# Taps of two channel chunks by small per-channel products, masks as wide products, and a new written-out order

## The chip, the cores and the metric

The kernel runs on one core of one Trainium2 chip. The metric is device time in microseconds (us) of one execution; lower is better. Three runs of the kernel before gave 263.95, 261.83 and 264.04, so its median is 263.95 us. One more execution, which took 262.47 us, was profiled.

## The reference

Two blocks stand one behind the other, each with its own LayerNorm and residual. Sequence length is 2048, model width D 512, state N 128, hidden width F 1376, batch 1.

```
dt = exp(log_dt);  logdA = dt*(A_re + 1j*A_im)
P  = exp(logdA[:, :, None] * l)                 # l = arange(2048), rounded to bf16
K  = einsum("dn,dnl,dn->dl", C, P, dt*B).real   # one filter of 2048 taps per channel
y  = irfft(rfft(u, 4096) * rfft(K, 4096))[:2048] + u*Dskip   # u = LN(x), a causal convolution
h  = x + y
z  = LN(LN(h));  g = gelu(z @ w1 + b1)
out = h + g @ w2 + b2
```

## The kernel before, in words

**Channels and stages.** The 512 channels are worked in four chunks (NCH) of 128. The filter taps are not computed one by one: a position l is split into a coarse part of NA = 20 entries (ROWS, table A) and a fine part of NB = 33 entries (table B), and a tap is a sum over the 128 states of a product of an A entry and a B entry, real part minus imaginary part. The stages, in the order of the data:

- *Small tables.* Inputs are loaded, transposed on TensorE (L712, L746), and turned into decay rates (th, L720 to L729), magnitudes (logarithms and exponentials on ACT, helper AC, L583) and phases (psi, gam). Helpers record the vector work, so one line stands for many operations: TS is L559 (DVE form) and L561 (tables and masks), TT is L571, STT is L576, evac copies a PSUM slot on ACT (L513) or on DVE (L515). A high and a low f16 half of each phase is made by split() (L685).
- *Exponentials.* bexps (L732) writes table B's magnitudes for all chunks, aexps (L941, L945; L949, L952) table A's.
- *Phases.* chain() adds phases step by step on PSUM (L986), ACT takes sine and cosine (L988), and DVE multiplies the magnitudes by them (L1006 to L1008, and L993, L994 for table A of chunks 2 and 3). It is called four times: B and A of chunks 0 and 1 (hf = 0), then B and A of chunks 2 and 3 (hf = 1). Each step of a chain waits for the sines of the step before.
- *Taps.* kgen (chunks 0 and 1): for each channel two products of 128x20 by 128x33 (L1030, L1031), four channels side by side in the array's columns; a chunk takes 256 of them and two evictions. kgen4 (chunks 2 and 3): four channels in one product of 128x128 by 128x132 (L1061, L1062), of which the diagonal blocks are used; a chunk takes 64 products and six evictions of up to 792 elements. For it table A of these chunks lies in another order (EA2, IA2, through dmaj), padded from 20 to 32 entries: a memset (L1301) zeroes the padding of one half and a DMA (L1339) copies it to the other.
- *Filter spectrum.* kspec (L1095) multiplies the taps by seven twiddle tables W[0..6], which are a sine table times row masks (28 products, L1318, on POOL or DVE); the result goes out to AK_d in device memory and comes back with its axes exchanged (kstage), and fstage (L912) transforms it on.
- *Input spectrum.* LayerNorm statistics (L871), normalized x in UN (L881), xspec (L893), fstage.
- *Product and back.* inverse() multiplies the spectra on DVE (L1135), transforms back (L1145), and a DMA transpose (turn, L1151) puts the result in place.
- *MLP.* tail() (L1214) adds the convolution to x and normalizes twice; mlp() multiplies by w1 (L1268), takes gelu on ACT (L1270), multiplies by w2 (L1290), and adds (L1292) and stores.

**What sets the order.** Nothing is scheduled by the compiler. Every operation is put on a list with its engines, its cost and its dependencies (Sched.add); ORDER (L166 to L203) is a list written out by hand that names the operations in the order in which they are issued, a negative number meaning the second engine that the operation allows. Sched.run walks that list, gives each operation its place on its engine, hands out the four PSUM slots, and puts filler matmuls (L1379) where it reckons that PE would idle. It also counts PE's instructions in blocks of 256, from 193 (L338 to L345). Each engine then works through its own list in order. SyncE (SP) issues nearly all transfers from one queue, in order too.

Of the kernel before, what the change touches and what calls it, by code (L numbers as in the profile page):

```python
# [384 lines left out]
def kernel(ctx, tc, A_u, A_A_re, A_A_im, A_B_re, A_B_im, A_C_re, A_C_im, A_log_dt, A_Dskip,  # L385
# [63 lines left out]
    EB0 = E0 + 2 * ASZ
    BA0 = E0 + 2 * ASZ + NCH * BSZ  # L450
    IB0 = BA0 + 2 * ASZ
    IA2 = at(BA0 + 2 * ASZ + NCH * BSZ, bf16, 2, 4, 32, 32)
    EA2 = at(IA2.hi, bf16, 2, 4, 32, 32)
    pos[0] = EA2.hi
    HF = 2 * ASZ + 2 * BSZ
# [18 lines left out]
    Kg = [take(bf16, NB, 2, 32), at(sc0 - 512, bf16, NB, 4, 2, 32)]
    zlo = take(bf16, NB, 2, 32).lo
    AK0 = take(bf16, 16, 2 * CW).lo
    XB = [at(lo + 16384, bf16, 8, 512) for lo in (E0, BA0)]
    PR = [[at(rest0 + 2048 * n, bf16, 8, CW) for n in range(4)], [take(bf16, 8, CW) for _ in range(2)] + [at(lo + 24576, bf16, 8, CW) for lo in (E0, BA0)]]
    Z = [[at(lo, bf16, P, 16) for lo in q] for q in ((zlo, sc0 + 8192), (EA2.lo + 11264, IA2.lo + 11264))]
# [1 line left out]
    EA = [at(E0 + c * ASZ, bf16, NA, CW) for c in range(2)]
    EB = [at(EB0 + c * BSZ, bf16, NB, CW) for c in range(NCH)]
    IA = [at(BA0 + c * ASZ, bf16, NA, CW) for c in range(2)]
    IB = [at(IB0 + c * BSZ, bf16, NB, CW) for c in range(NCH)]
# [935 lines left out]
```

## Time and profile before

| | |
|---|---|
| median of three runs | 263.95 us (261.83 to 264.04) |
| the profiled execution | 262.47 us |
| its span in the profile | 260.1 us |
| busy: PE / DVE / ACT / POOL | 230.3 / 183.3 / 176.8 / 61.8 us |
| share of the chain that ended last: PE / DVE / ACT | 57% / 25% / 11% |
| granted TensorE clock | 1.00 |

How to read the lines that follow. A line of the timeline has the start and the length in us, the engine, the line of the kernel, the operation with what it writes and reads, the count, and in brackets how long the engine sat idle before it and who released it. A group line has the busy time and the mean in ns of one instruction. A line of the windows has, per engine, its busy time in that stretch with the count of instructions, then the clock, the busy share of the DMA engines, and GB/s. PE is the matmul stream and PEld the weight loads that overlap it. "issue" is time in which an engine waited for nothing that the profile shows. Short matmuls overlap one another, so the time of one is read from the distance of their starts.

### The profile page before, as it was taken

How to read it: one execution, taken by the hardware profiler on the slowest of the kernel's cores; microseconds unless marked ns; L12 is line 12 of the kernel's file. 1: busy time of each engine (PE TensorE's matmuls, PEld its weight loads, DVE VectorE, ACT ScalarE, POOL GpSimd, SP SyncE). 2: the span in 40 equal slices, each digit the busy share in tenths (PEclk: the TensorE clock that was granted, in tenths of full speed). 3: DMA queues.
4: the chain of work that ended last, by engine and by line, in shares of the span. 5: the costliest groups of instructions: out<-in, count | busy, mean ns of one | idle time of the engine just before them, and what ended most of it. 6: DMA issues, size and time to landing. Idle time of an engine off the chain costs nothing.

```text
span 260.1 us, 7656 instructions
## 1 busy us (share of the span) xinstructions
PE 230.3 (89%) x3236; PEld 133.7 (51%) x3249; DVE 183.3 (70%) x368; ACT 176.8 (68%) x214; POOL 61.8 (24%) x234
## 2 busy tenths in 40 slices
PE   7215997888997999989999998899999999999994
PEld 3102673454876586444467765555553434444452
DVE  3999997999999964679899778974615676222021
ACT  2679989999977977578989956966514701762700
POOL 9930871699996000000000000000000000000000
PEclk9999999999999999999999999999999999999999
DMA  6940012000001247729835985560771040214202
GB/s 161 211 108 2 4 38 28 3 4 3 3 5 57 72 164 222 249 93 283 279 112 88 143 161 176 97 170 3 117 131 36 0 93 20 61 28 96 69 15 66
DMA packets 40371, 23.88 MB, mean 92 GB/s; under 512 B 25649, under 2 KB 37778, under 8 KB 40338
## 3 DMA queue, kind: packets, MB, share of 16 engines
q1 hardware_dynamic: 39746, 22.95, 36.8%
q10 hardware_dynamic: 592, 0.46, 0.8%
q8 instruction: 25, 0.41, 0.6%
q14 instruction: 8, 0.07, 0.1%
HBM read 10.03 MB, written 6.29 MB: 63 GB/s over the span
## 4 chain that ended last, share of the span: by engine, by line
PE 57%; DVE 25%; ACT 11%; issue 5%; POOL 0%; DVEq 0%; ACTq 0%; POOLq 0%
PE ps L1268 15%; PE ps L1290 15%; PE ps L1145 8%; PE ps L893 5%; ACT ar L988 4%; ACT ar L513 4%; DVE ar L871 4%; PE ps L912 4%; DVE ar L1007 3%; DVE ar L576 3%; DVE ar L571 2%; PE ps L1095 2%; PE ps L1061 2%; DVE ar L1008 2%; DVE ar L559 2%
## 5 line engine op out<-in xcount | busy, mean ns | idle before, releaser
L513 ACT CAST ar<-ps 128x1024 bf16<-128x1024 f32 (+3 forms) x72 | 65.2, 970 | 19.3 <-PE ps L1145 6.9
L1270 ACT ACTIVATE ar<-ps,ar 128x512 bf16<-128x512 f32 (+1 forms) x44 | 28.2, 686 | 36.7 <-PE ps L1268 36.6
L561 POOL TENSOR_SCALAR ar<-ar 128x128 bf16<-128x128 bf16 (+6 forms) x44 | 39.6, 921 | 7.6 <-ACT ar L583 7.3
L1290 PE MATMUL ps<-ar 128*128 128x512 bf16 (+3 forms) x180 | 39.1, 367 | 0.4
L1268 PE MATMUL ps<-ar 128*128 128x512 bf16 (+1 forms) x176 | 39.3, 379 | 0.0
L515 DVE CAST ar<-ps 128x1024 bf16<-128x1024 f32 (+2 forms) x28 | 30.6, 1113 | 11.9 <-ACT ar L513 4.0
L988 ACT ACTIVATE ar<-ps 128x1024 bf16<-128x1024 int16 x36 | 35.1, 1032 | 5.1 <-DVE ar L1007 1.6
L1135 DVE TENSOR_TENSOR ar<-ar 128x1024 bf16<-128x1024 bf16 x48 | 30.7, 687 | 10.3 <-PE ps L1145 9.9
L1292 DVE TENSOR_TENSOR ar<-ps,ar 128x512 bf16<-128x512 f32 (+1 forms) x17 | 11.1, 660 | 37.7 <-PE ps L1290 35.0
L1290 PEld LDWEIGHTS <-ar 128*128 128x128 bf16 (+1 forms) x187 | 17.9, 98 | 20.0 <-issue 0.8
L1268 PEld LDWEIGHTS <-ar 128*128 128x128 bf16 (+1 forms) x176 | 17.3, 100 | 20.5 <-issue 0.8
L986 PE MATMUL ps<-ar 128*32 128x256 f16 x560 | 21.4, 275 | 5.0 <-ACT ar L988 3.1
L1145 PEld LDWEIGHTS <-ar 64*128 64x128 bf16 x768 | 21.6, 94 | 5.4 <-issue 3.0
L1145 PE MATMUL ps<-ar 64*128 64x128 bf16 x768 | 23.9, 217 | 0.3 <-ACT ar L513 0.3
L986 PEld LDWEIGHTS <-ar 128*32 128x32 f16 x560 | 14.3, 97 | 12.5 <-issue 12.2
L912 PE MATMUL ps<-ar 128*64 128x512 bf16 (+1 forms) x160 | 17.7, 342 | 1.2 <-DMA ar<-AK_d 0.6
L732 ACT ACTIVATE ar<-ar 128x1024 bf16<-128x1024 f32 x16 | 15.6, 1041 | 3.2 <-DVE ar L559 3.2
L893 PE MATMUL ps<-ar 128*32 128x512 bf16 x256 | 16.0, 381 | 0.3 <-ACT ar L513 0.3
L576 DVE SCALAR_TENSOR_TENSOR ar<-ar 128x4 f32<-128x4 f32 (+5 forms) x44 | 14.2, 327 | 2.5 <-ACT ar L583 1.4
L583 ACT ACTIVATE ar<-ar 128x512 f32<-128x512 f32 (+8 forms) x18 | 11.9, 681 | 4.9 <-DMA ar<-in_A_log_dt_dram 1.8
L1008 DVE TENSOR_TENSOR ar<-ar 128x1024 bf16<-128x1024 bf16 x21 | 14.6, 719 | 0.0
L1007 DVE TENSOR_TENSOR ar<-ar 128x1024 bf16<-128x1024 bf16 x21 | 14.5, 716 | 0.1
(99 smaller groups left out, 318.6 us busy)
## 6 DMA issues: line engine op xcount, KB each, us to landing
ar<-AK_d SPq DMA_DIRECT2D x8, 512.0 KB, 5.6
ar<-in_A_u_dram SPq DMA_DIRECT2D x4, 512.0 KB, 9.2
AK_d<-ar SPq DMA_DIRECT2D x2, 1024.0 KB, 4.6
AK_d<-ar SPq DMA_DIRECT2D x4, 512.0 KB, 4.0
out_dram<-ar SPq DMA_DIRECT2D x30, 64.0 KB, 2.0
...
ar<-ar SPq DMA_DIRECT2D x1, 768.0 KB, 5.4
```

Of the source, the lines that this page charges most:

```text
L513: act.copy(out_fn(), in_fn())
L515: dve.tensor_copy(out_fn(), in_fn())
L561: en.tensor_scalar(a, b, f(s1), f(s2), op0, op1)
L893: pe.matmul(pst(p)[32 * cg:32 * cg + 32, 512 * z:512 * z + 512], lhsT=BD.ap()[:, 32 * f + 2 - 2 * jl:32 * f + 34 - 2 * jl], rhs=un[2 * (2 ...
L912: pe.matmul(pst(p)[64 * h:64 * h + 64, w * (k + r):w * (k + r) + w], lhsT=T.ap()[:, f, r, :], rhs=v[f:f + 1].ap()[:, 0, :], start=True, st ...
L986: pe.matmul(pst(p)[32 * g:32 * g + 32, 256 * j:256 * j + 256], lhsT=W2[DELTAS.index(d)].ap(), rhs=S2[g].ap()[:, ch0:ch0 + 256], start=Fals ...
L988: add("ACT", c_act(1024), lambda e, p=p, sc=sc, cs=cs: act.activation(swo(sc[cs]) if hf and kind == "B" else sc[cs].ap().rearrange("p a b ...
L1135: dve.tensor_tensor(o, a, b_[:, :, ::-1, :] if sw else b_, ALU.mult)
L1145: pe.matmul(pst(p)[:, 512 * h + 128 * k:512 * h + 128 * k + 128], lhsT=q.ap()[rows, 2 * k + r, :], rhs=TP[w].ap()[rows, f0 // 2 + k, :], s ...
L1268: pe.matmul(pst(p)[:fs, 512 * z:512 * z + 512], lhsT=w1s[dc].ap()[:, fc * P:fc * P + fs], rhs=ybuf.ap().rearrange("p (t c) k -> p c t k", ...
L1270: add("ACT", c_act(512, 1), lambda e, p=p, z=z, fc=fc, fs=fs: act.activation(hT.ap()[:fs, fc, :], pst(p)[:fs, 512 * z:512 * z + 512], ACT. ...
L1290: pe.matmul(pst(p)[:, 512 * z + c0:512 * z + c1], lhsT=hT.ap()[:fs, fc, 128 * t:128 * t + 128], rhs=w2s[fc].ap()[:fs, c0:c1], start=(fc == ...
```

## The change

It replaces kgen4 by kgen for chunks 2 and 3, so every chunk's taps come from per-channel products of 128x20 by 128x33, and the A tables of all chunks have one layout. With it go the padding memset and the padding DMA, the second arrangement of the sines (swo, swi), and the special multiplications of L993 and L994. The masks become one expanded table (mskx) and seven products of 512 elements in place of 28 of 128. Copies in split() and a few others may run on ACT as well as DVE (CP), and so may the normalization of x. One of two phase tables for TP goes; its third sine is taken in two halves from the first. The two Dskip additions of a pair of chunks become one. Buffers are laid out anew. ORDER is replaced as a whole (1,045 entries before, 1,000 after), and the cost of one case in Sched.run is raised by 0.3.

The core of the diff:

```diff
-    th = tL(f32, 5, 256)
...
-    TT(th[2], p, dtb, ALU.mult, n=256, ...)
-    add("DVE", c_dve(256, 1, True), th3, r=[p, dtb], w=[th[3]], hv=0)
-    TT(th[4], p, dtb, ALU.mult, n=256, ...)
-    TS(th[0:2], th[2:4], -1.0, None, ALU.mult, n=512, pr=0.35)
+    th = tM(f32, 4, 256)
+    for hf in range(2):
+        TT(th[2 + hf], p, dtb, ALU.mult, n=256, ...)
+        CP(th[hf], th[2 + hf], -1.0, pr=0.35)
...
+    def CP(o, i, m=1.0, n=None, iap=None, pr=None):
+        n = n if n is not None else (o.hi - o.lo) // SZ[o.dt]
+        def fn(e):
+            x = iap() if iap else i.ap()
+            if e == "ACT":
+                act.activation(o.ap(), x, ACT.Copy, scale=m)
+            else:
+                dve.tensor_scalar(o.ap(), x, m, None, ALU.mult)
+        add(("DVE", "ACT"), (c_dve(n, 2) + 0.02, c_act(n)), fn, r=[i], w=[o], pr=pr)
...
     def split(x, hl, pr, m=1.0):
-        TS(hl[0], x, m, None, ALU.mult, pr=pr)
+        CP(hl[0], x, m, pr=pr)
...
+    mskx = ct(bf16, 7, 4, 32)
+    mx = lambda e: (dve.tensor_copy if e == "DVE" else gp.tensor_copy)(mskx.ap()..., msk[0:28].ap().unsqueeze(2).to_broadcast([P, 28, 32]))
+    add(("POOL", "DVE"), (5.1, 1.0), mx, r=[msk], w=[mskx], pr=1.55, hv=1)
...
     for v in range(7):
-        for g in range(4):
-            PTS(W[v], valW, msk[4 * v + g:4 * v + g + 1], n=128, ...)
+        TT(W[v], valW, mskx[v], ALU.mult, n=512, mode=2, ..., eng="POOL")
...
-    add("DVE", 1.0, lambda e: dve.memset(pads(EA2), 0.0), w=[EA2], pr=0)
-    dma("SP", lambda: pads(IA2), lambda: pads(EA2), 786432, [EA2], [IA2], pr=3.45)
...
-            (kgen if q == 0 else kgen4)(c, 5.1 + 4 * c)
+            kgen(c, 5.1 + 4 * c)
+        add("DVE", c_dve(64), lambda e, q=q: dve.tensor_tensor(Kg[q][0].ap(), Kg[q][0].ap(), Dz[2 * q:2 * q + 2].ap(), ALU.add), ...)
...
-            add("DVE", c_dve(512, 4) + 0.13, ufn, r=[hs[8 * b + j], nw[3], nw[4]], w=[un[j]], ...)
+            add(("DVE", "ACT"), (c_dve(512, 4) + 0.13, c_act(512, 2)), ufn, r=[hs[8 * b + j], nw[3], nw[4]], w=[un[j]], ...)
```

In the kernel after, the lines that answer to those above are: products of the chain L985 and L986 (L984 their negation), phase matmuls L970 with the sines L972, taps L1008 and L1009, kspec L1045, xspec L886, fstage L905, inverse L1095 (matmuls) and L1085 (products), evac L500 (ACT) and L502 (DVE), w1 L1218, w2 L1240, fillers L1330.

More of the change, by code (lines that the diff above doesn't have):

```diff
@@ L321, in run @@
                     if a <= s < b:
-                        s, end = b, b + c
+                        s, end = b, b + c + 0.3
                 late = [a for a, _ in hold if s < a < end]
@@ L447 @@
     ASZ, BSZ = NA * CW * 2, NB * CW * 2
+    HF, A0 = 2 * ASZ + 2 * BSZ, 2 * ASZ
     E0 = pos[0]
[L449 to L455, printed above, removed]
+    BA0 = E0 + 2 * HF
+    pos[0] = BA0 + 2 * HF
     hs = [at(pos[0] + 1024 * n, bf16, 512) for n in range(16)]
     X0s = V(ar, pos[0] + 16384, bf16, (8, 512))
-    X0 = at(BA0 + HF, bf16, 16, 512)
+    X0 = at(BA0 + 2 * HF - 16384, bf16, 16, 512)
     pos[0] += 24576
@@ L473 @@
     XR = [VS(X0, c) for c in range(NCH)]
[L474 to L479, printed above, removed]
+    Kg = [at(pos[0], bf16, NB, 2, 32), at(sc0, bf16, NB, 2, 32)]
+    zlo = Kg[0].lo + 4224
+    WR = pos[0] + 11264
+    pos[0] = WR + 21248
+    AK0 = WR + 12288
+    X1 = at(E0, bf16, 16, 512)
+    PR = [[at(rest0 + 2048 * n, bf16, 8, CW) for n in range(4)], [at(BA0 + 26624 + 2048 * n, bf16, 8, CW) for n in range(4)]]
+    Z = [[at(lo, bf16, P, 16) for lo in q] for q in ((zlo, sc0 + 8448), (E0 + 16384, BA0 + 4096))]
     assert pos[0] <= NBYTES, pos[0]
[L481 to L484, printed above, removed]
+    EA, IA = ([at(lo + A0 * (1 - (c >> 1)) + ASZ * (c & 1), bf16, NA, CW) for c in range(NCH)] for lo in (E0, BA0))
+    EB, IB = ([at(lo + 2 * A0 + BSZ * c, bf16, NB, CW) for c in range(NCH)] for lo in (E0, BA0))
     ALL = slice(None)
@@ L540, in __call__ @@
             return v
-    tE = Tmp(BA0, BA0 + HF)
-    tL = Tmp(BA0 + HF, IA2.hi)
+    tE = Tmp(BA0 + A0, BA0 + A0 + HF)
+    tL, tM = Tmp(BA0 + A0 + HF, BA0 + 2 * HF), Tmp(BA0, BA0 + A0)
     ct = tL
@@ L595 @@
             dma("ACT", lambda: ldt.ap(), lambda: A_log_dt.partition_broadcast(P), 131072, [], [ldt], pr=0)
+    dtb = tE(bf16, 512)
     xv = x_dram.rearrange("(b q j h l) d -> b h q j (l d)", b=2, j=4, h=2, l=2)
@@ L621 @@
     NF = len(FLD)
-    fi, fsh, fmk = ct(i32, NF), ct(i32, NF), ct(i32, NF)
-    fm, fa, fv = ct(f32, NF), ct(f32, NF), ct(f32, NF)
+    fi, fsh, fmk = tE(i32, NF), tE(i32, NF), tE(i32, NF)
+    fm, fa, fv = tE(f32, NF), tE(f32, NF), ct(f32, NF)
     def fld_fn():
@@ L700 @@
     S.pr = 0.2
-    dtb = tE(bf16, 512)
     AC(dtb, ldt, ACT.Exp, tbl=True)
@@ L748 @@
         pas.append(lambda p=p, n=n: nat(pst(p, bf16)[:, 512 * n:512 * n + 512]))
-    crt, cit = tE(bf16, 512), tE(bf16, 512)
+    crt, cit = tL(bf16, 512), tL(bf16, 512)
     evac(by4(crt), pas[0], 512, [p], [crt])
@@ L781 @@
     S.pr = 0.5
-    psi, gam, wq, ps256 = tL(f32, 512), gr, tL(f32, 512), s2
+    psi, gam, wq, ps256 = tM(f32, 512), gr, tM(f32, 512), s2
     p, pa = tr("aim")
@@ L794 @@
     S.pr = 1.5
-    TPc = [at(Kg[0].lo, i32, 8, P), at(Kg[0].lo + 4096, i32, 8, P)]
+    TPc = at(Kg[0].lo, i32, 8, P)
     codD = ct(i32, 2, 16)
@@ L819 @@
     add("DVE", c_dve(928), lambda e: dve.tensor_reduce(msk.ap(), R.ap(), mybir.AxisListType.X, ALU.add), r=[R], w=[msk], pr=1.55)
+    mskx = ct(bf16, 7, 4, 32)
+    mx = lambda e: (dve.tensor_copy if e == "DVE" else gp.tensor_copy)(mskx.ap().rearrange("p v g c -> p (v g) c"), msk[0:28].ap().unsqueeze(2).to_broadcast([P, 28, 32]))
+    add(("POOL", "DVE"), (5.1, 1.0), mx, r=[msk], w=[mskx], pr=1.55, hv=1)
     wi = ct(i32, 4, 16)
@@ L872 @@
     stats(st, nw, 16, 1.0, EPS, 1.25, ln=True)
-    UN = [[X0s[j] for j in range(7)] + [at(zlo + 1024 * b, bf16, 512)] for b in range(2)]
+    UN = [X0s[j] for j in range(8)]
     def unorm(b, pr):
-        un = UN[b]
+        un = UN
         for j in range(8):
@@ L880, in ufn @@
                 sc_, bi_ = nw[3].ap()[:, s:s + 1], nw[4].ap()[:, s:s + 1]
-                dve.tensor_scalar(un[j].ap(), hs[s].ap(), sc_, bi_, ALU.mult, ALU.add)
-            add("DVE", c_dve(512, 4) + 0.13, ufn, r=[hs[8 * b + j], nw[3], nw[4]], w=[un[j]], pr=pr + 0.001 * (j // 4))
+                if e == "DVE":
+                    dve.tensor_scalar(un[j].ap(), hs[s].ap(), sc_, bi_, ALU.mult, ALU.add)
+                else:
+                    act.activation(un[j].ap(), hs[s].ap(), ACT.Identity, bias=bi_, scale=sc_)
+            add(("DVE", "ACT"), (c_dve(512, 4) + 0.13, c_act(512, 2)), ufn, r=[hs[8 * b + j], nw[3], nw[4]], w=[un[j]], pr=pr + 0.001 * (j // 4))
     def xspec(b, X, pr):
-        S.pr, un = pr, UN[b]
+        S.pr, un = pr, UN
         for f0 in range(0, 16, 2):
@@ L947, in aexps @@
                 add("PE", 1.75 if n < 3 else 0.88, fn, r=[HLt] + [WA[LV.index(LD[4 * n + j])] for j in range(4)] + ([HLg, Ih] if n < 3 else []), w=[p], new=[p] if n < 3 else [])
-                if hf == 0:
-                    add("ACT", c_act(1024), lambda e, p=p, n=n: act.activation(multi(E0 + 4 * n * 256, ASZ, bf16, 2, 4, CW).rearrange("p c a d -> p a c d"), pst(p).rearrange("p (a c d) -> p a c d", a=4, c=2), ACT.Exp),
-                        r=[p, TBL], w=[EA[c][4 * n + z] for c in range(2) for z in range(4)])
-                else:
-                    add("ACT", c_act(1024), lambda e, p=p, n=n: act.activation(dmaj(EA2, 4 * n).rearrange("p x a i -> p a x i"), pst(p).rearrange("p (a x i) -> p a x i", a=4, x=8), ACT.Exp),
-                        r=[p, TBL], w=[EA2])
+                add("ACT", c_act(1024), lambda e, p=p, n=n, hf=hf: act.activation(multi(EA[2 * hf].lo + 4 * n * 256, ASZ, bf16, 2, 4, CW).rearrange("p c a d -> p a c d"), pst(p).rearrange("p (a c d) -> p a c d", a=4, c=2), ACT.Exp),
+                    r=[p, TBL], w=[EA[2 * hf + c][4 * n + z] for c in range(2) for z in range(4)])
     nch = [0]
-    swo = lambda v: v.ap().rearrange("p a (c i g) -> p (a c) i g", c=2, g=4)
-    swi = lambda p: pst(p, i16).rearrange("p (b g i two) -> p b i g two", g=4, i=32, two=2)[:, :, :, :, 0]
     def chain(hf, kind, pr):
-        dm = hf == 1 and kind == "A"
         ch0 = 256 * hf
@@ L987, in chain @@
                 add("PE", 0.55 + (0 if gn else 0.45 if kind == "B" else 1.3), fn, r=[W2, S2, Wm, cst] + ([HLo, I16] if kind == "A" and gn == 0 else []), w=[p], new=[p] if gn == 0 else [])
-                add("ACT", c_act(1024), lambda e, p=p, sc=sc, cs=cs: act.activation(swo(sc[cs]) if hf and kind == "B" else sc[cs].ap().rearrange("p a b -> p (a b)"), swi(p) if hf and kind == "B" else pst(p, i16).rearrange("p (n two) -> p n two", two=2)[:, :, 0], ACT.Sin, scale=SINSC), r=[p, TBL], w=[sc[cs]])
+                add("ACT", c_act(1024), lambda e, p=p, sc=sc, cs=cs: act.activation(sc[cs].ap().rearrange("p a b -> p (a b)"), pst(p, i16).rearrange("p (n two) -> p n two", two=2)[:, :, 0], ACT.Sin, scale=SINSC), r=[p, TBL], w=[sc[cs]])
             mark = [("cg", kind, hf, gn)]
-            if dm:
-                E_, I_ = (lambda b0=b0: dmaj(EA2, b0)), (lambda b0=b0: dmaj(IA2, b0))
-                f_ = [lambda sc=sc, z=z: sc[z].ap().rearrange("p a (x i) -> p x a i", x=8) for z in range(2)]
-                add("DVE", c_dve(1024, 2), lambda e, E_=E_, I_=I_, f_=f_: dve.tensor_tensor(I_(), E_(), f_[0](), ALU.mult), r=[EA2, sc[0]], w=[IA2])
-                add("DVE", c_dve(1024, 2), lambda e, E_=E_, f_=f_: dve.tensor_tensor(E_(), E_(), f_[1](), ALU.mult), r=[EA2, sc[1]], w=[EA2] + mark)
-                continue
             Sx, Cx = (lambda sc=sc: sc[0].ap().rearrange("p e (c d) -> p c e d", c=2)), (lambda sc=sc: sc[1].ap().rearrange("p e (c d) -> p c e d", c=2))
@@ L1316 @@
     for v in range(7):
-        for g in range(4):
-            PTS(W[v], valW, msk[4 * v + g:4 * v + g + 1], n=128, oap=lambda v=v, g=g: W[v].ap()[:, :, 32 * g:32 * g + 32], pr=2.05)
-    Jk = ct(f32, 8, 64)
+        TT(W[v], valW, mskx[v], ALU.mult, n=512, mode=2, oap=lambda v=v: W[v].ap().rearrange("p t (g c) -> p t g c", g=4), aap=lambda: valW.ap().unsqueeze(2).to_broadcast([P, 4, 4, 32]),
+           bap=lambda v=v: mskx[v].ap().unsqueeze(1).to_broadcast([P, 4, 4, 32]), pr=2.05, eng="POOL")
+    Jk = at(Kg[0].lo + 4096, f32, 8, 64)
     POOL(1.1, lambda: gp.tensor_tensor(Jk.ap(), Jt.ap().unsqueeze(1).to_broadcast([P, 8, 64]), sk.ap().unsqueeze(2).to_broadcast([P, 8, 64]), ALU.mult), r=[Jt, sk], w=[Jk], pr=1.8, hv=1)
-    for r2 in range(2):
-        for r in range(2):
-            PTS(TPc[r2], Jk, 1.0, 16384.0 * (1 + r2 - r), op1=ALU.add, n=512, oap=lambda r=r, r2=r2: TPc[r2].ap().rearrange("p k (j r) -> p k j r", r=2)[:, :, :, r], pr=1.81 + 0.3 * r2)
+    for r in range(2):
+        PTS(TPc, Jk, 1.0, 16384.0 * (1 - r), op1=ALU.add, n=512, oap=lambda r=r: TPc.ap().rearrange("p k (j r) -> p k j r", r=2)[:, :, :, r], pr=1.81)
     chain(0, "B", 2)
@@ L1345 @@
         for c in (2 * q, 2 * q + 1):
-            (kgen if q == 0 else kgen4)(c, 5.1 + 4 * c)
+            kgen(c, 5.1 + 4 * c)
+        add("DVE", c_dve(64), lambda e, q=q: dve.tensor_tensor(Kg[q][0].ap(), Kg[q][0].ap(), Dz[2 * q:2 * q + 2].ap(), ALU.add), r=[Kg[q][0], Dz], w=[Kg[q][0]])
         for n, bs in enumerate(KB[q]):
@@ L1350 @@
     unorm(1, 9.6)
[L1351 removed]
+    xspec(1, X1, 9.7)
     for c in range(NCH):
```

85 lines of the change are left out of this document (24 added, 61 removed), and 71 rows, old and new, of the table ORDER.

## The prediction

> **What bounds the kernel now.** I read the page for the share of each engine, then the windows (busy time per stretch), the chain of waits in order of time, and the timeline of DVE, ACT and PE up to 113 us. The windows first:
>
> ```profile
> 45.00:90.00 45.00, 39.33 (x1135) 27.41 (x1138) 44.58 (x80) 39.91 (x47) 34.66 (x34) 1.00 0.07 21
> 90.00:105.00 15.00, 14.90 (x236) 10.47 (x227) 8.14 (x13) 12.16 (x13) 0.00 (x0) 1.00 0.57 183
> 220.00:240.00 20.00, 19.95 (x93) 9.18 (x93) 5.40 (x19) 10.40 (x16) 0.00 (x0) 1.00 0.27 57
> ```
>
> Columns: PE, PEld, DVE, ACT, POOL busy, then clock, DMA share, GB/s. From 45 to 90 us DVE is busy 44.58 of 45: the front end is DVE's. From 90 us on PE is busy almost without a gap: the rest is PE's. So two things count: when the front ends, and how much PE work is left then. The front's landmarks in the timelines:
>
> ```profile
> 5.66 0.64 DVE L726 TENSOR_TENSOR ar<-ps,ar 128x128 f32<-128x128 bf16 x2 [3.19 <-PE ps L712]
> 6.67 1.87 DVE L559 TENSOR_SCALAR ar<-ar 128x512 f32<-128x512 f32 x1
> 8.57 4.84 ACT L732 ACTIVATE ar<-ar 128x1024 bf16<-128x1024 f32 x5 [3.20 <-DVE ar L559]
> 43.56 1.42 DVE L576 SCALAR_TENSOR_TENSOR ar<-ar 128x512 f32<-128x512 f32 x2 [1.38 <-ACT ar L583]
> 47.45 1.30 DVE L1007 TENSOR_TENSOR ar<-ar 128x1024 bf16<-128x1024 bf16 x2
> 84.90 1.04 PE L1095 MATMUL ps<-ar 20*128 20x512 bf16 x16
> 85.88 1.26 PE L986 MATMUL ps<-ar 128*32 128x256 f16 x32
> 89.94 0.69 DVE L994 TENSOR_TENSOR ar<-ar 128x1024 bf16<-128x1024 bf16 x1
> ```
>
> The last phase matmul ends at 85.88 + 1.26 = 87.1; what PE does after it takes the other 173 us. The profiled execution took 262.47 us, 2.4 more than its span of 260.1, and lies 1.5 below the median of 263.95 (runs from 261.83 to 264.04). The sum is made against it.
>
> **The taps (kgen4 becomes kgen).** For chunks 2 and 3, 128 products of 128x132 (L1061, L1062) become 512 of 20x33 like those of chunks 0 and 1 (L1030, L1031). First and last rows of a run of each, 22 rows of 4 and 36 rows of 1:
>
> ```profile
> 66.55 0.27 PE L1030 MATMUL ps<-ar 128*20 128x33 bf16 x4
> 67.98 0.27 PE L1031 MATMUL ps<-ar 128*20 128x33 bf16 x4
> 90.68 0.29 PE L1061 MATMUL ps<-ar 128*128 128x132 bf16 x1
> 93.03 0.23 PE L1062 MATMUL ps<-ar 128*128 128x132 bf16 x1
> ```
>
> The 88 small ones start over 1.49 us (to the next at 68.04), 17 ns each; the 36 large ones over 2.42, 67 ns each. So 512 x 17 = 8.7 us against 128 x 67 = 8.6: nothing on PE. Their evictions shrink:
>
> ```profile
> L515 DVE CAST ar<-ps 128x792 bf16<-128x792 f32 x6 | 5.8, 981 | 2.5 <-ACT ar L513 1.9 <-PE ps L1062 0.6
> L515 DVE CAST ar<-ps 128x264 bf16<-128x264 f32 x2 | 0.9, 434 | 2.6 <-PE ps L1062 2.6
> L513 ACT CAST ar<-ps 128x792 bf16<-128x792 f32 x4 | 3.3, 843 | 0.8 <-PE ps L1062 0.8
> L513 ACT CAST ar<-ps 128x726 bf16<-128x726 f32 x2 | 1.5, 766 | 0.0
> L513 ACT CAST ar<-ps 128x330 bf16<-128x330 f32 x2 | 0.9, 438 | 0.0
> ```
>
> Twelve evictions (10.0 us) become four (2.4). But they lie after 90 us, where PE is busy anyway: PE can gain only its small waits. Term D: -0.5 (0 to -1.5).
>
> **The front, up to DVE's first product (47.45).** The order listing gives what stands on DVE before that product in both kernels; the prices are those of
>
> ```profile
> L561 DVE TENSOR_SCALAR ar<-ar 128x512 f32<-128x512 f32 x4 | 1.7, 422 | 0.1
> 21.91 0.43 DVE L559 TENSOR_SCALAR ar<-ar 128x512 f16<-128x512 f32 x1
> L571 DVE TENSOR_TENSOR ar<-ps,ar 128x512 f32<-128x512 bf16 x4 | 2.5, 677 | 0.0
> L819 DVE TENSOR_REDUCE ar<-ar 128x29 f32<-128x928 f32 x1 | 1.1, 1114 | 0.0
> L561 DVE TENSOR_SCALAR ar<-ar 128x128 f16<-128x128 bf16 x11 | 3.0, 368 | 0.0
> ```
>
> Gone: the two of L726 (0.64); the negation of 512 (1.87), of which a 256 stays (about 0.3) and a 256 goes to ACT; one f16 copy to ACT (0.43); one TPc table of 512 (0.42); one 128-wide scaling (0.37). New: one PSUM copy of 512 (about 0.65, by the L571 that reads PSUM) and the mask expansion of 896 elements, not in the trace: between 0.5 (a 512 copy's pace and a little) and 1.1, as L819 reduces 928; I take 1.0. Sum -1.8. The idle 1.38 at 43.56 goes too: DVE waits there for ACT, which has run exponentials since 8.57, released by the negation. In the new order that release comes from a 256 piece on each engine, about 1.5 us earlier, and the products from which ACT's logarithms start are ahead of the phase work. So the first product comes about 3.1 earlier (1.5 if ACT is not earlier). The removed padding memset (1.34) ran while DVE waited for inputs anyway: 0, as DVE is idle 3.19 right after it.
>
> **The front, from there to the last product (89.94).**
>
> ```profile
> L561 DVE TENSOR_SCALAR ar<-ar 128x128 bf16<-128x128 bf16 x4 | 1.2, 298 | 0.0
> L561 POOL TENSOR_SCALAR ar<-ar 128x128 bf16<-128x128 bf16 x24 | 26.4, 1113 | 7.3 <-ACT ar L583 7.3
> L881 DVE TENSOR_SCALAR ar<-ar 128x512 bf16<-128x512 bf16 x16 | 6.1, 423 | 0.0
> L515 DVE CAST ar<-ps 128x1024 bf16<-128x1024 f32 x20 | 24.0, 1221 | 6.9 <-PE ps L912 3.7 <-ACT ar L513 2.1 <-PE ps L893 0.3
> L1007 DVE TENSOR_TENSOR ar<-ar 128x1024 bf16<-128x1024 bf16 x21 | 14.5, 716 | 0.1
> L1239 ACT ACTIVATE ar<-ar 128x512 bf16<-128x512 bf16 x11 | 8.2, 817 | 0.0
> ```
>
> The 26 pairs of products stay, at the same price. On DVE four mask products go (-1.2), three of the seven wide ones come (0.35, half of L1007, to 0.7 each: +1.5), three normalizations of x move to ACT or later (-1.25), two evictions of 1024 come later (-2.4), two tap evictions come from ACT (0.98 and 0.43: +1.4), the Dskip additions save 0.2: together -2.15. POOL's 24 mask products of 1.11 become four wide ones; W is first read by L1095, behind the phase work, so this frees nobody. ACT gains 0.6 in this stretch (two normalizations of 0.8, priced by L1239, and one split sine in, two tap evictions of 0.77 and 0.44 out) and was busy 39.91 of 45; DVE 44.58. After the change they are at about 42.4 and 40.5, and each waits for the other within every group of phases, so I take not 2.15 but 0.9. Term A: -3.1 - 0.9 = -4.0 (-5.3 to -1.5).
>
> **What is left to PE after the last phase matmul.** By the listing the same instructions (512 taps for 128; 25 fillers in both), but also the 16 products of L1095 that now come after it (1.04 at 84.90). Term B: +1.0. The padding's DMA goes:
>
> ```profile
> 82.04 0.73 SPq L525 DMA_DIRECT2D ar<-ar  x1
> 90.58 6.45 SPq L525 DMA_DIRECT2D AK_d<-ar  x2
> ar<-ar SPq DMA_DIRECT2D x1, 768.0 KB, 5.4
> ```
>
> It was issued at 82.04 and landed 5.4 later, before the AK writes of 90.58, so it delayed none: 0. The new order on SP puts the two AK_d11 writes ahead of four transposes, and their reads behind; the products that need them (L912 x32) are 70 us of PE work after the front, so they are covered.
>
> **Fetching PE's instructions.** The change adds 768 PE instructions: the listing has 6,500 before and 7,258 after.
>
> ```profile
> q8 instruction: 25, 0.41, 0.6%
> 75.13:77.89 2.76, 2.69 (x133) 1.00 0.03 6
> 77.89:81.89 4.00, 3.17 (x131) 1.00 0.01 4
> 81.88 0.25 PE L1031 MATMUL ps<-ar 128*20 128x33 bf16 x1 [0.66 <-issue]
> 93.19 1.49 PE L1095 MATMUL ps<-ar 20*128 20x256 bf16 x48
> 98.88 0.98 PE ps L893 x16
> ```
>
> 25 packets of 16 KB for 6,500 instructions are blocks of 256, about 128 weight-load and matmul pairs; run() counts them too, from 193 in steps of 256. The two windows are two such blocks in the tap stretch: one passes in 2.76 us, the next takes 4.00 with an idle 0.66 at its end that no engine released, two instructions short of the boundary. So a block of taps can wait for its instructions. After the last phase matmul the new order has blocks of 4.4, 3.1, 3.4, 3.7 and 3.3 us of PE work (taps at 17 ns, L1095 at 65, or 31 where 256 wide, L893 at 61); before, each block there had 7 us or more. At 2.76 a block nothing is lost, at 4.0 0 + 0.9 + 0.6 + 0.3 + 0.7 = 2.5. Term C: +1.5 (0 to 2.5), nearer to the 4.0 since DMA is busy 0.57 there and was at 0.01 in the row.
>
> The Trainium skill (Runtime: NRT & Kernel Launch, Instruction fetch mechanics) also has blocks of 256 instructions, and calls the cost of crossing a boundary mostly hidden; the 0.66 disagrees at that one boundary. By the page C is 0 and the sum -3.5, a rival below.
>
> **The sum:** A -4.0, B +1.0, C +1.5, D -0.5: -2.0. 262.5 - 2.0 = 260.5 us. Ends: -5.3 + 1.0 + 0 - 1.5 = -5.8 (256.7) and -1.5 + 1.0 + 2.5 + 0 = +2.0 (264.5).
>
> **Rivals.** (1) The gain is larger: the blocks come ahead of their use at 2.76 us each, as in the first of the two windows (C 0), or DVE's whole 2.15 counts. -3.5 gives 259.0, with both -4.7. For it: DVE has no slack in the front; against: the 0.66. Chance 0.25. (2) No gain: ACT cannot follow, the first product is only 1.5 earlier and the chain saves nothing: -1.5 + 1.0 + 1.5 - 0.5 = +0.5, 263.0. For it: ACT's 39.91 of 45. Chance 0.15. (3) Slower, by one mechanism: the tap blocks after 87 us become bound by their instructions, since their packets share the DMA engines with the AK writes and reads. At 5 us a block the five lose 0.6 + 1.9 + 1.6 + 1.3 + 1.7 = 7.1 and the time is 266; the gain is gone from about 4.25 a block on, where they lose 3.5. For it: the 4.00 on idle DMA; against: that block also held phase matmuls that waited for ACT. Chance 0.20. The forecast, -0.5 to -3.5, has 0.40; its own range is 259.0 to 262.0.
>
> **Chances.** A measurement of this kernel tells about 1% from no change. The forecast lies 0.75% under the profiled execution and 1.3% under the median, so half of its 0.40 counts as faster, with rival 1: 0.45. The other half and rival 2: 0.35. Rival 3: 0.20. The range 256.7 to 264.5 leaves out rival 3 and little else.
>
> **What would show it.** Right: DVE's first product (L985 after) near 44 us, the last phase matmul (L970) near 83, ACT's exponentials from about 7; PE busy from there, with idle put down to issue inside the tap runs (L1008, L1009) of 1 to 2 us in all; 28 or 29 instruction packets. Wrong: a tap run after the front slower than 17 ns a product with no issue gap (the taps cost PE more than I say), DVE idle on ACT's sines for over 3 us in the front (term A), or PE idle on AK reads before the first product of inverse() (the transfers are not covered).

## The result, and the profile after

Nine runs of each kernel on one chip: before 262.63 us median (261.83 to 264.04), after 265.62 us (264.35 to 266.34). The ratio is 1.0093, 95% interval 1.0064 to 1.0122: slower by 0.9%, where 260.5 us and a gain were forecast. The profiled execution of the changed kernel took 265.93 us, its span is 263.8.

The same three windows as before the change (columns as there):

```profile
45.00:90.00 45.00, 35.83 (x1053) 24.38 (x1045) 43.02 (x69) 36.07 (x40) 15.80 (x15) 0.92 0.01 3
90.00:105.00 15.00, 12.93 (x485) 9.48 (x481) 6.37 (x9) 10.23 (x10) 0.00 (x0) 1.00 0.44 143
220.00:240.00 20.00, 20.00 (x94) 9.13 (x93) 4.98 (x17) 7.92 (x12) 0.00 (x0) 1.00 0.27 57
```

DVE is still busy nearly all of 45 to 90, 43.02 of 45, but with 69 instructions where it had 80. PE did 3.5 us less there, and its granted clock is 0.92. POOL is busy less than half as long as before. The landmarks of the front, from the timelines of ACT, DVE and PE:

```profile
6.83 3.90 ACT L721 ACTIVATE ar<-ar 128x1024 bf16<-128x1024 f32 x4 [0.31 <-DVE ar L558]
38.99 0.69 DVE L563 SCALAR_TENSOR_TENSOR ar<-ar 128x512 f32<-128x512 f32 x1 [0.54 <-ACT ar L570]
43.85 1.29 DVE L985 TENSOR_TENSOR ar<-ar 128x1024 bf16<-128x1024 bf16 x2
87.87 0.40 PE L970 MATMUL ps<-ar 128*32 128x256 f16 x7 [0.29 <-issue]
89.12 1.28 DVE L986 TENSOR_TENSOR ar<-ar 128x1024 bf16<-128x1024 bf16 x2
```

DVE's first product comes at 43.85, 3.6 us earlier than before (47.45). The last phase matmul ends at 88.27, 1.1 later than before (87.14). So a head start of 3.6 us and another 1.1 are lost between those two lines: that stretch took 39.7 us and takes 44.4. Here is where, first DVE, then POOL, over the same time:

```profile
45.80 2.25 DVE L985 TENSOR_TENSOR ar<-ar 128x1024 bf16<-128x1024 bf16 x2
47.97 1.63 DVE L986 TENSOR_TENSOR ar<-ar 128x1024 bf16<-128x1024 bf16 x1
49.53 0.68 DVE L985 TENSOR_TENSOR ar<-ar 128x1024 bf16<-128x1024 bf16 x1
52.56 3.08 DVE L985 TENSOR_TENSOR ar<-ar 128x1024 bf16<-128x1024 bf16 x2
55.57 0.88 DVE L986 TENSOR_TENSOR ar<-ar 128x1024 bf16<-128x1024 bf16 x1
56.77 1.63 DVE L986 TENSOR_TENSOR ar<-ar 128x1024 bf16<-128x1024 bf16 x1
58.92 2.12 DVE L986 TENSOR_TENSOR ar<-ar 128x1024 bf16<-128x1024 bf16 x2
...
45.92 3.14 POOL L558 TENSOR_TENSOR ar<-ar 128x512 bf16<-128x512 bf16 x2
51.08 2.47 POOL L548 TENSOR_SCALAR ar<-ar 128x1024 int32<-128x1024 int32 x1
53.51 1.58 POOL L558 TENSOR_TENSOR ar<-ar 128x512 bf16<-128x512 bf16 x1
56.64 1.21 POOL L558 TENSOR_TENSOR ar<-ar 128x512 bf16<-128x512 bf16 x1
57.84 2.66 POOL L548 TENSOR_SCALAR ar<-ar 128x1024 int32<-128x1024 int32 x1
```

A product of DVE that stands alone takes 0.68 us (third line), a pair 1.28. The six other DVE lines are longer by 0.97, 0.95, 1.80, 0.20, 0.95 and 0.84: together 5.7 us. Except for the 0.20, each lies beside one of POOL's four wide mask products (L558) or its two 1024-wide code instructions (L548). The forecast for this stretch was -0.9 and it came out at +4.7; the difference of 5.6 is about those 5.7 us. (Smaller changes lie in it as well, such as 0.9 us in which DVE waited for ACT's sines.) If the 1.80 is split like its neighbours, 0.95 beside the mask and 0.85 beside the code, some 3.8 us lie beside the masks and 1.7 beside the codes. Half of the codes' part is new as well: in the kernel before one code ran ahead of the first product, in 1.19 us, and only the other ran beside a pair of DVE, which took 1.63 where such a pair takes 0.85:

```profile
30.87 1.19 POOL L561 TENSOR_SCALAR ar<-ar 128x1024 int32<-128x1024 int32 x1
68.12 1.63 DVE L1006 TENSOR_SCALAR ar<-ar 128x1024 bf16<-128x1024 bf16 x2
```

DVE counts as busy all that time, so no list of idle times shows it: it shows in the length of instructions whose shape has not changed.

### The profile page after: what moved, and what is told of

Read it like the earlier page. It is cut to its first block, busy times and chain, and to the rows that moved or that the text cites. A ratio compares the mean times of both kernels' runs of the same rounds, so it can differ in the third digit from the quotient of the medians.

```text
span 263.8 us, 8395 instructions
## 1 busy us (share of the span) xinstructions
PE 232.1 (88%) x3628; PEld 133.6 (51%) x3628; DVE 181.8 (69%) x357; ACT 174.9 (66%) x212; POOL 42.5 (16%) x214
## 4 chain that ended last, share of the span: by engine, by line
PE 64%; ACT 19%; DVE 12%; issue 4%; POOL 0%; ACTq 0%; DVEq 0%; POOLq 0%
PE ps L1218 15%; PE ps L1240 15%; PE ps L1095 7%; ACT ar L500 6%; PE ps L889 6%; ACT ar L721 5%; PE ps L970 4%; ACT ar L941 3%; PE ps L1009 3%; PE ps L1008 3%; DVE ar L986 3%; DVE ar L985 3%; PE ps L908 3%; PE ps L1045 2%; PE ps L1164 2%
## 5 line engine op out<-in xcount | busy, mean ns | idle before, releaser
L500 ACT CAST ar<-ps 128x1024 bf16<-128x1024 f32 (+3 forms) x63 | 57.4, 986 | 20.9 <-PE ps L1095 8.5
L1220 ACT ACTIVATE ar<-ps,ar 128x512 bf16<-128x512 f32 (+1 forms) x44 | 29.3, 687 | 42.2 <-PE ps L1218 35.7
L502 DVE CAST ar<-ps 128x1024 bf16<-128x1024 f32 (+2 forms) x29 | 32.7, 1136 | 18.0 <-PE ps L889 5.5
L972 ACT ACTIVATE ar<-ps 128x1024 bf16<-128x1024 int16 x36 | 35.7, 1027 | 8.3 <-DVE ar L986 3.8
L1218 PE MATMUL ps<-ar 128*128 128x512 bf16 (+1 forms) x176 | 40.0, 379 | 0.0
L1240 PE MATMUL ps<-ar 128*128 128x512 bf16 (+3 forms) x187 | 39.7, 367 | 0.0
L1085 DVE TENSOR_TENSOR ar<-ar 128x1024 bf16<-128x1024 bf16 x48 | 30.7, 686 | 6.1 <-PE ps L1095 5.6
L970 PE MATMUL ps<-ar 128*32 128x256 f16 x560 | 24.3, 292 | 9.0 <-ACT ar L972 7.8
L1240 PEld LDWEIGHTS <-ar 128*128 128x128 bf16 (+1 forms) x187 | 18.1, 98 | 20.0 <-issue 0.4
L1218 PEld LDWEIGHTS <-ar 128*128 128x128 bf16 (+1 forms) x176 | 17.1, 100 | 20.6 <-issue 1.2
L1095 PEld LDWEIGHTS <-ar 64*128 64x128 bf16 x768 | 21.7, 94 | 6.0 <-issue 3.3
L1095 PE MATMUL ps<-ar 64*128 64x128 bf16 x768 | 24.1, 216 | 0.3 <-ACT ar L500 0.2
L970 PEld LDWEIGHTS <-ar 128*32 128x32 f16 x560 | 14.9, 102 | 17.9 <-issue 17.4
L1009 PE MATMUL ps<-ar 128*20 128x33 bf16 x512 | 20.6, 248 | 1.9 <-issue 1.9
L1008 PE MATMUL ps<-ar 128*20 128x33 bf16 x512 | 20.6, 248 | 0.3 <-ACT ar L500 0.3
L985 DVE TENSOR_TENSOR ar<-ar 128x1024 bf16<-128x1024 bf16 x26 | 20.0, 792 | 1.0 <-ACT ar L972 0.9
L986 DVE TENSOR_TENSOR ar<-ar 128x1024 bf16<-128x1024 bf16 x26 | 20.1, 798 | 0.1
L1008 PEld LDWEIGHTS <-ar 128*20 128x20 bf16 x512 | 18.3, 123 | 2.5 <-issue 1.5
L908 PE MATMUL ps<-ar 128*64 128x512 bf16 (+1 forms) x160 | 17.6, 341 | 1.8 <-ACT ar L500 1.2
L1009 PEld LDWEIGHTS <-ar 128*20 128x20 bf16 x512 | 18.0, 124 | 2.2 <-issue 1.9
L889 PE MATMUL ps<-ar 128*32 128x512 bf16 x256 | 17.9, 403 | 0.0
```

Of the source, the lines that this page charges most:

```text
L500: act.copy(out_fn(), in_fn())
L502: dve.tensor_copy(out_fn(), in_fn())
L889: pe.matmul(pst(p)[32 * cg:32 * cg + 32, 512 * z:512 * z + 512], lhsT=BD.ap()[:, 32 * f + 2 - 2 * jl:32 * f + 34 - 2 * jl], rhs=un[2 * (2 ...
L970: pe.matmul(pst(p)[32 * g:32 * g + 32, 256 * j:256 * j + 256], lhsT=W2[DELTAS.index(d)].ap(), rhs=S2[g].ap()[:, ch0:ch0 + 256], start=Fals ...
L972: add("ACT", c_act(1024), lambda e, p=p, sc=sc, cs=cs: act.activation(sc[cs].ap().rearrange("p a b -> p (a b)"), pst(p, i16).rearrange("p ...
L1008: pe.matmul(o, lhsT=Ar.ap()[:, :, d], rhs=Br.ap()[:, :, d], start=True, stop=False, tile_position=(0, 32 * g))
```

## The experiments

**Theory 1:** POOL, when it reads much from SBUF, holds up DVE's products, and the four wide mask products ate the head start. **Theory 2:** the new order costs the time, on PE or ACT, or in the fetch of tap instructions, and the long DVE lines are not POOL's doing. Each ratio below is to runs of the kernel before on the same chip.

**e1_w_on_dve.** In ORDER, 226, 227, 229 and 230 (four of the seven products W) are given to their second engine, in place:

```diff
-    ..., 230, ..., 227, ..., 226, ..., 229, ...
+    ..., -231, ..., -228, ..., -227, ..., -230, ...
```

> The changed kernel, with its four wide mask products that POOL does (W, 128x512 bf16, two inputs) given to DVE at the same place of the order. Theory 1 (a wide two-input product on POOL holds up DVE's two-input products): the four DVE products of 1.6 us and the like between 46 and 58 us go back to 0.65, 4 x 0.95 = 3.8 us less; DVE pays 4 x 0.36 = 1.4 us for the masks; the last phase matmul comes at 85.9 instead of 88.3 and the time is 263.2. Theory 2 (the long DVE instructions are not POOL's doing, the new order costs the time): the masks only come on top, 265.6 to 267.0.

Ratio 0.9924 (0.9890 to 0.9957), 260.98 us. DVE and PE in its timeline:

```profile
45.80 1.29 DVE L985 TENSOR_TENSOR ar<-ar 128x1024 bf16<-128x1024 bf16 x2
47.01 0.69 DVE L986 TENSOR_TENSOR ar<-ar 128x1024 bf16<-128x1024 bf16 x1
49.37 2.32 DVE L986 TENSOR_TENSOR ar<-ar 128x1024 bf16<-128x1024 bf16 x2
53.43 1.26 DVE L984 TENSOR_SCALAR ar<-ar 128x1024 bf16<-128x1024 bf16 x1
60.02 0.41 DVE L558 TENSOR_TENSOR ar<-ar 128x512 bf16<-128x512 bf16 x1
83.27 0.40 PE L970 MATMUL ps<-ar 128*32 128x256 f16 x7 [0.29 <-issue]
```

The pair at 45.80 is back to 1.29 and the last phase matmul ends at 83.67. The gain over the changed kernel, 1.7% or 4.4 us, is more than the 2.4 expected; the half clock of the changed kernel, to which e9 below comes, is gone as well. Two lines stay long, the 2.32 and the 1.26, both beside POOL's codes.

**e3_w_all_pool** and **e5_before_wide_w** dose the cause. The first gives all seven products to POOL (codes -229, -232, -233 become 228, 231, 232). The second puts them into the kernel before, and nothing else of the change:

```diff
+    mx = lambda e: (...).tensor_copy(mskx..., msk[0:28]...)      # expanded once, on DVE
-        for g in range(4):
-            PTS(W[v], valW, msk[4 * v + g:4 * v + g + 1], n=128, ...)
+        TT(W[v], valW, mskx[v], ALU.mult, n=512, mode=2, ..., eng="POOL")    # 4 on POOL, 3 on DVE
```

> The changed kernel with all seven wide mask products on POOL, none on DVE: the suspected cost nearly doubled. Theory 1: three more long DVE products, 3 x 0.95 less 3 x 0.36 saved on DVE = +1.8 us, 267.4. Theory 2: DVE is relieved of 1.1 us, 264.5 to 265.6.

> The kernel before with this one part of the change: masks expanded once on DVE and made by seven wide products, four on POOL, three on DVE, everything else as it was. Theory 1: +3.8 us of long DVE products, +0.6 for the expansion, -1.0 for the drag of the narrow ones: 266.0, with DVE products of about 1.6 us right after the first product. Theory 2: 262 to 263, since POOL has less to do and nobody waits for it.

e3: 1.0219 (1.0176 to 1.0261), 269.21 us, where theory 1 said 267.4: the right way, and 1.8 us more. e5: 1.0109 (1.0075 to 1.0142), 265.80 us, where theory 1 said 266.0. In e3 the 26 products of L986 have a mean of 876 ns (798 in the changed kernel); those of L985 have 760 (792), but two negations (L984) now stand beside masks and take 1.38 and 1.37 where they took 0.70 and 0.47. The trace of e3 is of its fastest execution, with a span of 265.0, 1.2 more than the changed kernel's, so where the rest of its loss lies is not shown. In e5 the very first pair of the front is long, as no pair there was before:

```profile
L986 DVE TENSOR_TENSOR ar<-ar 128x1024 bf16<-128x1024 bf16 x26 | 22.0, 876 | 0.1
```

```profile
47.45 2.25 DVE L1010 TENSOR_TENSOR ar<-ar 128x1024 bf16<-128x1024 bf16 x2
```

So this one part of the change, alone, makes the kernel before as slow as the whole change does.

**e2_w_narrow.** The changed kernel with W made by the old 28 narrow instructions (PTS as in the lines taken out above), 24 on POOL behind its other work.

> The changed kernel with the masks made as in the kernel before: 28 TENSOR_SCALAR of 128 columns, 24 on POOL behind all its other work, 4 on DVE (their inputs moved to a place that stays free until then). Theory 1: a one-input instruction on POOL hardly holds up DVE (products of 0.77 beside 0.68 in the kernel before), so 3.8 us of long products go and about 1 us of small drag comes: 262.8, and the only long products left are those beside POOL's two 1024-wide int32 instructions. Theory 2: 265.6, or more if the masks come too late for the spectrum of K (they end near 85 us).

Ratio 0.9935 (0.9907 to 0.9963), 261.01 us. POOL is busy 18 us longer than in the changed kernel, and the kernel is faster by 1.6%: POOL's busy time is not what counts.

**e6_codes_early.** On top of e1, operations 28, 29, 30 (an iota and the two codes) go ahead in ORDER, behind 224, to where POOL stands idle:

```diff
-    ..., 28, ..., 29, ..., 30, ...
+    ..., 224, 28, 29, 30, ...
```

> The kernel of the masks on DVE (e1_w_on_dve) with POOL's iota and two 1024-wide int32 instructions (codT, L548) moved ahead in POOL's order to 34.8 us, where POOL stands idle for 5.3 us. Theory 1 (whatever POOL reads from SBUF in the chain holds up DVE): the two long DVE entries left there (L986 x2 of 2.32, L984 of 1.26) go back to 1.28 and 0.41, 1.9 us less, 259.1; what POOL holds up at 35 to 40 us instead is mostly hidden, since DVE waits there for ACT. Rival (only two-input products on POOL hold DVE up, and those two DVE entries are long for another reason): no change, 261.0.

Ratio 0.9843 (0.9807 to 0.9879), 258.71 us, the fastest of those that leave nothing out.

```profile
35.88 2.37 POOL L548 TENSOR_SCALAR ar<-ar 128x1024 int32<-128x1024 int32 x2
36.15 0.94 DVE L563 SCALAR_TENSOR_TENSOR ar<-ar 128x16 int32<-128x16 int32 x1
37.02 1.26 DVE L548 TENSOR_SCALAR ar<-ar 128x16 int32<-128x16 int32 x2
47.68 0.89 DVE L985 TENSOR_TENSOR ar<-ar 128x1024 bf16<-128x1024 bf16 x1
52.70 0.42 DVE L984 TENSOR_SCALAR ar<-ar 128x1024 bf16<-128x1024 bf16 x1
```

L984 is back to 0.42. Both codes together take 2.37 us, where one took 2.47 or 2.66 beside DVE's products: the hold goes both ways. One-input instructions hold DVE up too, so the rival (two inputs only) falls. The codes are not free at their new place: the lines at 36.15 and 37.02 take 0.23 and 0.36 in e1, so 1.6 us are lost there. The first product still comes at 43.90, as in e1 (43.85), because DVE has room before it: in e1 it waits 0.52 for ACT, and one instruction there takes 1.39 beside the iota, where it takes 0.43 in e6, which has the iota elsewhere. From e1, DVE and then POOL:

```profile
40.44 1.39 DVE L548 TENSOR_SCALAR ar<-ar 128x512 f32<-128x512 f32 x1
40.52 1.03 POOL L649 IOTA ar<- 128x1024 int32 x1
```

**e10_pool_writes, e11_pool_one_input, e12_pool_two_inputs.** Into e6's POOL list go four instructions that serve nobody, alike but for what they read:

```diff
+    spare = at(WR + 12544, bf16, 512)        # 1536 for the memset
+    for n in range(4):
+        gp.memset(spare, 0.0)  |  gp.tensor_scalar(spare, cst, 1.0, ...)  |  gp.tensor_tensor(spare, cst, cst, mult)
```

> The best kernel so far (e6_codes_early: masks on DVE, codes early, ratio 0.984) with four idle POOL instructions that only write (memsets of 128x1536 bf16, some 1.5 us each) where the wide products stood in POOL's order. Theory 1a (DVE is held up by what POOL reads from SBUF): no DVE product is longer, ratio 0.984. Rival 1b (any busy POOL holds DVE up): four products longer by about 0.95, +3.8 us, ratio 0.998.

> As e10_pool_writes, but the four idle instructions are TENSOR_SCALAR with one input of 128x512. If the hold goes by the elements that POOL reads (0.09 us beside 128, 0.2 beside 2 x 128, 0.95 beside 2 x 512 and beside 1024 int32, so near 0.9 ns each), four times 0.45: +1.8 us, ratio 0.991. If one-input instructions are nearly free whatever their width (the 0.09 of the 128 columns): +0.4 us, ratio 0.986.

> As e10_pool_writes, but the four idle instructions are TENSOR_TENSOR with two inputs of 128x512: the masks' own form, with nobody waiting for their result. By elements read: 4 x 0.95 = +3.8 us, ratio 0.998, perhaps up to 1 us more if PE starves and its clock falls. If the masks cost their time in another way than by holding DVE up (their results come late, their order), nothing: 0.984.

Ratios 0.9872 (0.9830 to 0.9914), 0.9910 (0.9875 to 0.9945), 1.0003 (0.9970 to 1.0036): against e6, 0.8, 1.8 and 4.2 us more, where 0, 1.8 and 3.8 were expected. The first is not told apart from 0. One fence for each, in that order:

```profile
47.67 0.68 DVE L985 TENSOR_TENSOR ar<-ar 128x1024 bf16<-128x1024 bf16 x1
52.65 1.17 DVE L984 TENSOR_SCALAR ar<-ar 128x1024 bf16<-128x1024 bf16 x1
...
45.95 2.82 POOL L1269 MEMSET ar<- 128x1536 bf16 x2
52.12 1.42 POOL L1269 MEMSET ar<- 128x1536 bf16 x1
```

```profile
47.47 1.09 DVE L986 TENSOR_TENSOR ar<-ar 128x1024 bf16<-128x1024 bf16 x1
...
45.96 2.06 POOL L1269 TENSOR_SCALAR ar<-ar 128x512 bf16<-128x512 f16 x2
```

```profile
47.90 1.52 DVE L986 TENSOR_TENSOR ar<-ar 128x1024 bf16<-128x1024 bf16 x1
...
45.96 2.92 POOL L1269 TENSOR_TENSOR ar<-ar 128x512 bf16<-128x512 f16 x2
```

A DVE product beside a POOL memset takes 0.68, as alone. Beside a one-input instruction of 512 it takes 1.09, beside a two-input one 1.52: 0.41 and 0.84 longer. The memset is not wholly free: the L984 at 52.65, a copy with a factor, took 0.76 longer beside one, as the TENSOR_SCALAR at 40.44 in e1 did beside the iota, which reads nothing either.

**e9_after_fillers.** The changed kernel, masks on POOL as they were, with fillers in one gap of PE and operation 327 behind 286:

```diff
+MORE = {286: 14}
...
+            for _ in range(MORE.get(i, 0)):
+                order.append(d)        # d is a filler matmul
```

> The changed kernel, its masks on POOL as they were, with 14 filler matmuls of 128x512 put into PE's wait near 57 us and the first phase group of the second half's B chain moved behind that wait. Theory (PE, starved by the long DVE products, fell under some share of work and was granted half its clock from about 61 to 68 us, which slowed the phase matmuls and cost the chain about 2 us more): the granted clock is 1.00 from 60 to 75 us and the time is 263.6. Rival (the clock falls for another reason, or the half clock costs nothing because DVE is the bound): 265.6 or more.

Ratio 1.0068 (1.0038 to 1.0098), 264.59 us. The windows from 57 us of the changed kernel, then one of e9:

```profile
57.00:60.00 3.00, 0.75 (x31) 0.56 (x21) 3.00 (x4) 1.48 (x2) 3.00 (x2) 1.00 0.00 0
62.00:66.00 4.00, 3.56 (x50) 1.90 (x49) 3.96 (x8) 3.50 (x5) 0.00 (x0) 0.50 0.02 4
```

```profile
62.00:66.00 4.00, 2.82 (x70) 1.70 (x66) 4.00 (x8) 3.82 (x6) 0.00 (x0) 1.00 0.02 4
```

The cause of the low clock here is shown: PE worked 0.75 of 3.00 us while DVE was held up and then got half its clock; with fillers it keeps 1.00. What that half clock cost is not settled. The medians differ by 1.0 us, the ratios by 0.7, the spans by 1.6 (263.8 to 262.2), and the intervals overlap; the fillers also ran on for half a microsecond too long. In the two traces little of it lies in the front: the last phase matmul of e9 ends at 87.93, 0.3 earlier than in the changed kernel, where the expectation had 2. The other 1.2 us lie behind it, where the changed kernel has a second stretch at half clock, after a wait of PE on issue, and e9 has none. From e9, then twice from the changed kernel:

```profile
87.00 0.93 PE L977 MATMUL ps<-ar 128*32 128x256 f16 x25 [0.27 <-issue]
...
103.00:105.00 2.00, 0.25 (x13) 0.12 (x14) 1.22 (x1) 0.00 (x0) 0.00 (x0) 1.00 0.50 161
106.00:108.00 2.00, 2.00 (x49) 1.36 (x41) 0.00 (x0) 0.77 (x1) 0.00 (x0) 0.50 0.03 8
```

**e7_small_ak, e8_half_taps, e13_taps_later** ask about term C, the fetch of PE's instructions.

```diff
e7  -    dma("SP", ... D...[cp], ... ak.ap()[:, 8 * cp:8 * cp + 8, :], ...)
e7  +    dma("SP", ... D...[cp][:, :, 0:128], ... ak.ap()[:, 8 * cp:8 * cp + 8, 0:128], ...)    # first AK only, its reads likewise
e8  -    pe.matmul(o, lhsT=Ai..., rhs=Bi..., start=False, stop=True, ...)
e8  +    if c < 2: pe.matmul(o, lhsT=Ai..., rhs=Bi..., start=False, stop=True, ...)
e13 -    ..., 455, 456, ..., 457, ..., 506, 458, 459, -508, 520, 424, -461, ..., 462, ..., 463, ..., 508, ...
e13 +    ..., 506, 455, 456, 457, -508, 520, 458, 459, -461, 424, ..., 508, 462, 463, ...
```

> The kernel of the masks on DVE with only a quarter of each row of the first AK transfer written and read back (128 of 512 columns; the rest of K's spectrum is left stale, so the output is not the reference's). It is a look at one gap: in e1_w_on_dve PE's weight loads pause for 1.76 us in the tap run near 98 us, three before the boundary of a block of 256 instructions, while 2 MB of AK leave. If the pause is the fetch of instructions held back by that transfer, it shrinks to under 0.6 us. If the fetch is late by itself, it stays between 1.5 and 2.0 us.

> The kernel of the masks on DVE without the second (imaginary) product of the taps of the two channels that come after the front: 256 of 512 matmuls there and their weight loads are left out, two blocks of 256 instructions; the output is not the reference's. If taps cost what PE works on them, 256 x 17 ns = 4.4 us go: 256.6. If the blocks are bound by their fetch (the excess over PE's work in the five blocks from 2753 to 3777 is about 2.5 us in e1_w_on_dve), the pause goes with them: 6 to 6.7 us less, 254.5.

> e6_codes_early with the last tap run (four groups of 16 taps products and more, with their evictions and the product that needs them) moved behind twelve spectrum matmul groups of x, so that instructions that PE works on longer stand where the 2 MB of AK leave. Theory (the pause of 1.61 us in e6_codes_early at 98 us is a fetch held back by that transfer, and work with fewer instructions per us covers it): the pause shrinks under 0.6 and 1.0 us goes, ratio 0.980. Rival (the wait moves to the tap run's new place, or the later spectrum of K delays its own transfer): 0.984 or more.

PE's waits from 85 to 105 us (time in all, times, longest) and the transfer that runs there, of e1 and then of e7:

```profile
PE ps L1009 <- issue: 2.0, 2, 1.5
...
AK_d<-ar SPq DMA_DIRECT2D x2, 1024.0 KB, 6.6
```

```profile
PE ps L1009 <- issue: 0.4, 2, 0.2
...
AK_d<-ar SPq DMA_DIRECT2D x2, 256.0 KB, 3.6
```

With a quarter of the data the longest such wait falls from 1.5 to 0.2 us (one execution of e7, 258.90 us): the wait comes from the AK transfer. That the transfer does it by holding back PE's instructions is argued: no engine released PE, the place is a boundary of 256, and the instruction queue's packets lie further apart beside the large transfer (after one between 92 and 93 us, the next comes between 97 and 98 in e1, and between 95 and 96 in e7).

e8: ratio 0.9736 (0.9699 to 0.9772), 1.9% or 5.0 us under e1, and 4.5 by the spans: nearer to the 4.4 of PE's work than to the 6 to 6.7 of a fetch-bound run. It does not settle this alone, since the pause goes with the taps (PE's waits on issue from 85 to 105 us are 0.4) and two waits for DVE of 0.9 in all come in its place. That PE waits on issue for 2.0 us in all in that stretch of e1, and for 1.7 of L1009 in the changed kernel, speaks more plainly against tap blocks that are bound by their instructions as a whole.

e13 was a miss: 0.9889 (0.9855 to 0.9924), where 0.980 was expected; that it is slower than e6 the intervals, which overlap, do not show. The move changed nothing at the pause, which stands on L908 with this same line in e6 and in e13:

```profile
PE ps L908 <- issue: 1.0, 1, 1.0
```

## Why the prediction was wrong, by its steps

**The failed step** is in the front's second half: "POOL's 24 mask products of 1.11 become four wide ones; W is first read by L1095, behind the phase work, so this frees nobody", with "the 26 pairs of products stay, at the same price". It priced POOL's work by who waits for its result, and gave it 0. Its price is what it takes from DVE while it runs: e1 to the changed kernel, 4.4 us; alone in the kernel before (e5), 2.9 us; at seven products instead of four (e3), another 3.3 us. The chain's -0.9 became +4.7. The two codes on POOL, which the prediction does not name and which the new order puts both into the chain, belong to the same step: e6 gains 2.1 us by taking them out.

With the masks on DVE (e1) the time is 0.9924 of before, -2.0 us, which is the forecast's own sum, but partly by luck. By the traces the first product is 3.6 earlier (forecast 3.1), the chain takes 0.1 more (39.8 against 39.7, forecast -0.9) and what follows 1.9 more (forecast 2.0), in all -1.6. That chain pays 1.6 us for four masks on DVE, which the forecast did not have, and still some 1.9 for the codes.

**Two rows of the kernel before gave the hint**, and the prediction quotes one: POOL's 24 mask instructions of 128 columns have a mean of 1113 ns, while nine of the same width and engine, earlier and with another type, have 357:

```profile
L561 POOL TENSOR_SCALAR ar<-ar 128x128 f16<-128x128 bf16 x9 | 3.2, 357 | 0.2
```

Three times as long beside DVE's products was a hint that the two engines share something.

**The first product** (A, first part): forecast 3.1 earlier, measured 3.6; right. The expansion of the masks, not in the trace and taken as 1.0, took 0.62. ACT's exponentials start at 6.83 (about 7 forecast), the wait for ACT shrank from 1.38 to 0.54.

**After the last phase matmul** (B, C, D: +1.0 + 1.5 - 0.5 = +2.0): 263.8 - 88.27 = 175.5 us against 173.0 before, +2.6 before rounding; in e1, with the clock at 1.00, 258.5 - 83.67 = 174.8, +1.9. The sum is right in e1; the 0.7 more of the changed kernel goes with its second stretch at half clock, which no run took out alone. C came as one pause at the AK transfer (1.7 us) and not as small waits at several blocks, and 28 instruction packets came, as forecast. Tap products of the changed kernel start 17 ns apart (76 from 91.42 to 92.72), as forecast. B and D were not measured alone.

**The rivals.** Rival 3 gave 266, near the 265.6 measured, but by tap blocks bound by their instructions after 87 us; that needs 7.1 us of waits, and PE's wait on issue in the tap runs is 1.7. In e7 the pause is worth 1.6 us (2.0 less 0.4), about what C had. Its number was right for the wrong reason. Rival 1 (a larger gain, -3.5 to -4.7) has about e6's number (-4.1), but e6 gets it by moving the codes, with the pause still there. Rival 2 (ACT cannot follow) fails too: the two product lines L985 and L986 waited for ACT's sines 0.9 us in all. None of the three named what POOL does to DVE, so the range of 256.7 to 264.5 had no case for it; and none of the three signs of being wrong came (slower tap products, over 3 us on ACT's sines, PE idle on AK reads).

**What the Trainium skill says of it.** The Trainium skill (SBUF — State Buffer, Who interferes with whom) states that a DVE instruction with two SBUF inputs contends with a GpSimd instruction that reads SBUF and not with one that only writes, and that a tensor_scalar of DVE in its two-port mode contends with both. The runs agree: 1.09 and 1.52 beside reads, 0.68 beside memsets, and the L984 of 1.17 beside a memset (that it runs in that mode no trace here shows). It also states that whoever issues first has the shared ports for the whole instruction. The runs do not settle that: DVE's products lost 0.41 beside instructions of 1.03 and 0.84 beside instructions of 1.46, but these lengths hold POOL's own waiting for DVE too. Beside the codes of e6, 1.19 each, DVE's small instructions lost 0.71 and 0.90, and the second of the two lines ends with the codes (38.28 and 38.25).
